# Four products at two Strassen levels in layer one's second gate/up pass, with most second-level weight sums on GpSimd

## The chip, the cores and the metric

The kernel runs on one core of a Trainium2 chip. The metric is device time of one execution in microseconds (us); lower is better.

## What is computed

Two identical layers, each an attention block without softmax (A) followed by a gated block (B), over x of 2048 rows and 1024 columns. The same weights serve both layers. Cut to what matters here:

```python
def _B_ref(x, w_gate, w_up, w_down):
    g = jnp.einsum("bsd,df->bsf", x, w_gate)   # 1024 -> 3584
    u = jnp.einsum("bsd,df->bsf", x, w_up)
    h = g * u
    return jnp.einsum("bsf,fd->bsd", h, w_down)

x = x + _A_ref(_layernorm(x), A_wqkv, A_wo)
x = x + _B_ref(_layernorm(x), B_w_gate, B_w_up, B_w_down)
x = x + _A_ref(_layernorm(x), A_wqkv, A_wo)
x = x + _B_ref(_layernorm(x), B_w_gate, B_w_up, B_w_down)
```

## The kernel before

All of it is one instruction stream per engine, written out by Python. Each operation names the bytes of SBUF and the PSUM banks that it reads and writes, and a planner turns these into semaphore waits. Every engine executes its stream in order: TensorE (PE), VectorE (DVE), ScalarE (ACT), GpSimd (POOL), and SyncE (SP), from whose queue all DMAs are issued.

In a gated block the 2048 rows are done as two halves of 1024. A half is one gate/up pass and then one down-projection. A gate/up pass runs over 14 pairs of *units*. A unit is a block of 256 columns of w_gate or of w_up, the other unit of the pair the same columns of the other matrix. The product of a unit with the half's 1024 rows is done by Strassen's scheme in Winograd's form: instead of eight block products it takes seven, called 1 to 7, each with a 512 x 128 block (or a sum of blocks) of weights and a 512 x 512 block (or a difference) of the input: four matmuls of 512 columns for each unit. The first-level weight sums (for products 5, 6, 7, 3) are made once, in layer one's first pass, stored in `w_scratch` and loaded from there afterwards.

A product of the pair can be taken at a *second level*. The blocks of both units together are then split again into seven smaller products, 14 matmuls of 256 columns instead of 8 of 512. That needs second-level sums of the weights (four 128 x 256 blocks a product, `sp`), second-level differences of the input (once a pass, `tp_ops`), and more additions while results leave PSUM. `L2SETS` says for each (layer, pass) which products are taken so: none in layer one's first pass, 1 and 5 in its second, all of 1, 5, 3, 2 in both of layer two's. Layer one's second pass makes the second-level weight sums of all four products, for itself and for layer two, and stores them in `sp_scratch`; layer two only loads them.

The order of a pass is written out by hand as a string of tokens in `ORDERS`, which is repeated for each pair. `P`, `D` and a product's number with A or B are a product's matmuls for the first or second unit; `M` are the operations that combine and multiply results into h; two digits are steps of a second-level product (`11` the first matmuls of product 1, `16`, `17` the next two; `25`, `35` an addition on DVE), `F` folds one term in. `S` makes (layer one) or loads (layer two) second-level weight sums. `Ra` and `Rb` issue the loads of one unit each, in a ring of five slots (`ring_issue`): `Ra` of a pair loads the second unit of the next pair. `T0` and `T1` are ticks, at which other work is put in; in layer one's second pass that is the layer norm of layer two for eight tiles of 128 rows (`ticks1`). A token with `'` belongs to the pair before, one with `+` to the next. The first tokens of a pass, as far as they are in `early`, are put among the last matmuls of the down-projection ahead.

Lines of the profile that matter here: matmuls of 512 columns L1037, of 256 columns L1104, of the down-projection L1312. DVE's tensor-tensor operations all have L668 (the helper `tt`), its evictions from PSUM L671 (`stt`), the joins of second-level products L1122. ACT's evictions are L1042, L1051 and, of second-level products, L1147; its copies from bank to bank L1067 and L1119. Layer norm is L432, L434 and L452 on DVE and L435, L437 on POOL. L583, L585 (DVE) and L792 (POOL) belong to the projections of block A, L800 (DVE) and L809 (POOL) to its norm. DMAs are issued at L406, transposing ones at L524.

Of the kernel before, what the change touches and what calls it, by code (L numbers as in the profile page):

```python
# [180 lines left out]
def build_kernel(nc, A_x, A_wqkv, A_wo, B_w_gate, B_w_up, B_w_down, out):  # L181
# [11 lines left out]
    NNORM = 14  # L193
    YACT = True

    L2SETS = {(False, 0): "", (False, 1): "15", (True, 0): "1532", (True, 1): "1532"}
    ORDERS = {
# [4 lines left out]
    }  # L202
# [104 lines left out]
    with ExitStack() as es:  # L307
# [97 lines left out]
        def dma(dst_ap, src_ap, wr, key, rd=()):  # L405
            P.add("sp", lambda e: e.dma_start(dst_ap, src_ap), rd=rd, wr=wr, dma_sem=key)  # L406
# [231 lines left out]
        def ring_issue():  # L638
            n = RG["n"]
            if n >= 2 * NPASS:  # L640
                return
            RG["n"] = n + 1
            o = r_slot(n)[0][0]
            ps_, u = divmod(n, NPASS)
            sl = (n + 1) % NR
            if u < NU:
                j, m = unit_jm(u)
                src = wgu_v[m][:, :, j * 256:(j + 1) * 256]
                if RG["first"] and ps_ == 0:
                    dma(vb(o, 2048).rearrange("p (k c) -> p k c", c=256), src, R(o, 4096), KRR[sl])  # L650
                else:
                    dma(vb(o + 1024, 1024).rearrange("p (k c) -> p k c", c=128), src[:, :, 0:128], R(o + 1024, 2048), KRR[sl])
                    dma(vh(o + 3072, 2048), wscr[u], R(o + 3072, 4096), KRT[sl], rd=R(V_S + u * 32, 32))
                    dma(vb(o, 512).rearrange("p (k c) -> p k c", c=128), src[:, 4:8, 128:256], R(o, 1024), KRS[sl])
                return
            q, hf = divmod(u - NU, 2)
            q = DPROD[q]
            js = slice(hf * 7, hf * 7 + 7)
            if q in "123":
                e, d = {"1": (0, 0), "2": (1, 0), "3": (1, 1)}[q]  # L660
                dma(vb(o, 7 * 512).rearrange("p (j c) -> p j c", c=512), wd_v[:, js, e, d * 512:(d + 1) * 512], r_slot(n, 0, 7168), KRR[sl])
            else:
                t = {"5": 0, "6": 1, "7": 2, "4": 3}[q]
                dma(vh(o, 7 * 512).rearrange("p (j c) -> p j c", c=512), tscr[t][:, js, :], r_slot(n, 0, 7168), KRR[sl],
                    rd=R(V_D + hf * 7 * 32, 7 * 32))

        def tt(out, a, b, op, rd, wr, prd=()):
            P.add("dve", lambda e: e.tensor_tensor(out=out, in0=a, in1=b, op=op), rd=rd, wr=wr, prd=prd)  # L668

        def stt(out, a, sc, b, rd, wr, prd=(), op1=ALU.add):  # L670
            P.add("dve", lambda e: e.scalar_tensor_tensor(out=out, in0=a, scalar=sc, in1=b, op0=ALU.mult, op1=op1), rd=rd, wr=wr, prd=prd)  # L671
# [62 lines left out]
        def wt_h(o):  # L734
            return vh(o, 512).rearrange("p (k c) -> p k c", c=128)

        def wt_n(o, h, c):
            v = vb(o + 2048 * h, 1024).rearrange("p (k c) -> p k c", c=256)[:, :, 128 * c:128 * c + 128]
            return v, _seg(o + 2048 * h, 4, 512, 256 * c, 256 * c + 256)

        def prep_s(n):
            o = r_slot(n)[0][0]
            sv = [wt_h(o + 4096 + i * 1024) for i in range(4)]
            (a11, r11), (a12, r12), (a21, r21), (a22, r22) = [wt_n(o, h, c) for c in range(2) for h in range(2)]
# [264 lines left out]
        def layer_B(lnp, nxt, first):  # L1009
            is_last = nxt is None  # L1010

            def pair(ps_, p, l2):
# [5 lines left out]
                for ab_ in range(2):  # L1018
                    n = ps_ * NPASS + 2 * p + ab_
                    o = r_slot(n)[0][0]  # L1020
                    if first and ps_ == 0:
                        w = {"1": wt_n(o, 0, 0), "2": wt_n(o, 1, 0), "4": wt_n(o, 1, 1)}
# [151 lines left out]
                    so = O_SS["3"]  # L1174
                    tt(vh(so, 1024), vh(so, 1024), vh(O_CP, 1024), ALU.add, R(so, 2048) + R(O_CP, 2048), R(so, 2048))

                def sums(g, mode):
                    if mode == "load":
                        sp_load(ps_, p, g)
                        return  # L1180
                    v, rp, rv = sp_place(ps_, p, g)
                    sp = [v[:, i].rearrange("p (b c) -> p b c", b=2) for i in range(4)]
                    ws = []
                    for u in units:
                        o_ = r_slot(u["n"])[0][0]
                        if g == "12":
                            ws.append((vb(o_ + 1024, 1024).rearrange("p (b k c) -> p b k c", b=2, k=2), R(o_ + 1024, 2048)))
                        else:
                            ws.append((vh(o_ + 3072, 2048).rearrange("p (b k c) -> p b k c", b=4, k=2)[:, 0::3], R(o_ + 3072, 1024) + R(o_ + 6144, 1024)))
                    (wA, rA), (wB, rB) = ws  # L1190
# [19 lines left out]
            def gateup(ps_, ticks, l2):  # L1210
# [7 lines left out]
                def emit(it, tk):  # L1218
# [19 lines left out]
                        c["c22"](x) if tk[1] == "5" else c["fmul"](tk[1], x)  # L1238
                    elif tk[0] == "S":
                        if not jit:  # L1240
                            c["sums"](SPG[tk[1] == "5"], "make" if first else "load")
                    elif tk[0] == "F":
                        c["fold"]()
                    elif tk[0] == "T":
# [6 lines left out]
                    else:  # L1251
# [258 lines left out]
```

## Time and profile before

| what | value |
|---|---|
| median of 3 runs | 1464.54 us (1464.37 to 1464.82) |
| the profiled execution | 1464.57 us, span 1462.8 us |
| granted TensorE clock | 1.00 |
| layer one's second gate/up pass | about 497 to 660 us of the span |
| busy in 500 to 650 us | DVE 129.58, ACT 83.85, POOL 6.97 of 150 us |
| DMA share in 500 to 650 us | 1.01 |

The views of the profile used below: the page (one line per engine, the chain that ended last), the groups of instructions by line, which give the count, the busy time and the mean of one and then the idle time before them with the instruction that ended it; the windows, with each engine's busy time in a stretch; and the timeline, one row for each instruction or run of equal ones, with its start and its length. A busy engine is not an engine at its peak: matmuls overlap, so their rate is read from the distance of their starts.

### The profile page before, as it was taken

To read this page: it belongs to the slowest core of one execution; us is meant where nothing else is said; L and a number is where in the kernel's file an instruction comes from. 1 tells how busy PE (TensorE), PEld (TensorE's weight loads), DVE (VectorE), ACT (ScalarE), POOL (GpSimd) and SP (SyncE) were. 2 spreads that over 40 slices of the span, in tenths; PEclk is the share of its full clock that TensorE was granted. 3 is DMA by queue.
4 is the path that set the end of the run, shared out by engine and by line. 5 is a ranking of instruction groups with operands and counts; after the bars stand their busy time and mean duration, and the time that the engine had idled before them with its cause. 6 is when DMAs were issued, how large, how long until landed. Compare 5 with 4: busy or idle time off the path is not lost.

```text
span 1462.8 us, 20720 instructions
## 1 busy us (share of the span) xinstructions
PE 1453.9 (99%) x7830; PEld 751.8 (51%) x7830; DVE 1090.1 (75%) x1990; ACT 572.0 (39%) x1178; POOL 225.8 (15%) x239
## 2 busy tenths in 40 slices
PE   8999999999999999999999999999999999999999
PEld 3444444444444555554444444456666446666544
DVE  7986888777757699865578769879877575777653
ACT  3332355333300255550023323567776005777400
POOL 4553632000000000000034337300000000000000
PEclk9999999999999999999999999999999999999999
DMA  6133667988875799975374337679986768888642
GB/s 230 37 94 107 138 131 188 278 259 259 279 253 190 259 274 291 281 242 187 127 231 123 106 108 152 152 211 272 284 258 199 243 221 240 263 264 241 217 167 94
DMA packets 370931, 298.11 MB, mean 204 GB/s; under 512 B 234640, under 2 KB 323472, under 8 KB 370832
## 3 DMA queue, kind: packets, MB, share of 16 engines
q1 hardware_dynamic: 370832, 296.80, 69.6%
q8 instruction: 61, 1.00, 0.3%
q14 instruction: 38, 0.31, 0.1%
HBM read 218.63 MB, written 54.53 MB: 187 GB/s over the span
## 4 chain that ended last, share of the span: by engine, by line
PE 99%; DMA 1%; DVE 0%; ACT 0%; SPq 0%; issue 0%
PE ps L1037 30%; PE ps L1312 23%; PE ps L780 15%; PE ps L1104 15%; PE ps L862 8%; PE ps L954 7%; DMA arena<-in_A_wqkv_dram 1%; PE ps L902 0%; PE ps L874 0%; SPq L406 0%; PE ps L538 0%; DVE arena L668 0%; ACT arena L540 0%; PE ps L886 0%; DVE arena L671 0%; DVE arena L960 0%
## 5 line engine op out<-in xcount | busy, mean ns | idle before, releaser
L671 DVE SCALAR_TENSOR_TENSOR arena<-ps,arena 128x512 f16<-128x512 f32 (+2 forms) x508 | 340.4, 686 | 195.1 <-PE ps L1312 140.8
L1037 PE MATMUL ps<-arena 128*128 128x512 f16 x2016 | 478.5, 379 | 0.0
L668 DVE TENSOR_TENSOR arena<-arena 128x512 f16<-128x512 f16 (+4 forms) x624 | 308.8, 520 | 54.1 <-ACT arena L1147 46.4
L1312 PE MATMUL ps<-arena 128*128 128x512 f16 (+1 forms) x1568 | 340.9, 379 | 0.0
L1037 PEld LDWEIGHTS ps<-arena 128*128 128x128 f16 (+1 forms) x2016 | 192.3, 98 | 186.7 <-ACT arena L1042 13.6
L1104 PE MATMUL ps<-arena 128*128 128x256 f16 x1960 | 259.4, 273 | 0.8 <-DVE ps L1122 0.5
L1312 PEld LDWEIGHTS ps<-arena 128*128 128x128 f16 x1568 | 153.4, 98 | 183.1
L1104 PEld LDWEIGHTS ps<-arena 128*128 128x128 f16 (+1 forms) x1960 | 190.9, 98 | 83.3 <-DVE ps L1122 3.8
L780 PE MATMUL ps<-arena 128*128 128x512 bf16 x1024 | 223.7, 379 | 3.2 <-ACT arena L540 1.1
L1042 ACT ACTIVATE arena<-ps 128x512 f16<-128x512 f32 x224 | 133.8, 597 | 110.6 <-PE ps L1037 108.6
L582 ACT ACTIVATE arena<-ps 128x512 f32<-128x512 f32 x128 | 76.4, 597 | 231.5 <-PE ps L780 220.1
L780 PEld LDWEIGHTS ps<-arena 128*128 128x128 f16 x1024 | 99.6, 98 | 122.0 <-DMA arena<-in_A_wqkv_dram 1.6
L1119 ACT COPY ps<-ps 128x256 f32<-128x256 f32 x168 | 61.8, 368 | 204.0 <-PE ps L1104 201.4
L435 POOL TENSOR_SCALAR arena<-arena 128x1 f32<-128x1 f32 x64 | 27.2, 425 | 643.0 <-DVE arena L434 643.0
L862 PE MATMUL ps<-arena 128*128 128x512 bf16 x512 | 115.4, 379 | 0.0
L954 PE MATMUL ps<-arena 128*128 128x512 bf16 x512 | 111.0, 379 | 0.0
L1067 ACT COPY ps<-ps 128x512 f32<-128x512 f32 x112 | 64.2, 573 | 90.6 <-PE ps L1037 52.4
L1122 DVE TENSOR_TENSOR ps<-ps,arena 128x256 f32<-128x256 f32 x168 | 70.7, 428 | 33.6 <-PE ps L1104 16.7
L432 DVE BATCH_NORM_STATS2 arena<-arena 128x6 f32<-128x512 bf16 x128 | 88.2, 689 | 8.2 <-DMA arena<-in_A_x_dram 6.0
L585 DVE SCALAR_TENSOR_TENSOR arena<-ps,arena 128x512 bf16<-128x512 f32 x128 | 88.5, 692 | 4.4
L809 POOL TENSOR_TENSOR arena<-arena 128x1024 f16<-128x1024 f32 x32 | 79.3, 2478 | 72.9 <-DVE arena L807 71.7
L792 POOL TENSOR_TENSOR arena<-arena 128x512 f32<-128x512 f32 x60 | 74.7, 1249 | 87.1 <-DVE arena L585 85.7
(51 smaller groups left out, 705.3 us busy)
## 6 DMA issues: line engine op xcount, KB each, us to landing
arena<-w_scratch SPq DMA_DIRECT2D x84, 512.0 KB, 5.4
arena<-t_scratch SPq DMA_DIRECT2D x32, 896.0 KB, 5.7
arena<-sp_scratch SPq DMA_DIRECT2D x56, 512.0 KB, 6.0
arena<-in_B_w_down_dram SPq DMA_DIRECT2D x24, 896.0 KB, 5.8
w_scratch<-arena SPq DMA_DIRECT2D x28, 512.0 KB, 6.6
sp_scratch<-arena SPq DMA_DIRECT2D x28, 512.0 KB, 4.1
arena<-in_A_wqkv_dram SPq DMA_DIRECT2D x12, 1024.0 KB, 8.0
arena<-in_B_w_gate_dram SPq DMA_DIRECT2D x42, 256.0 KB, 5.4
```

The source lines that it names most:

```text
L432: P.add("dve", (lambda h: lambda e: e.bn_stats(st[j][:, 6 * h:6 * h + 6], x_res[:, i, (D // 2) * h:(D // 2) * (h + 1)]))(h), rd=r_x(i, (D ...
L585: P.add("dve", lambda e: e.scalar_tensor_tensor(out=dst_ap, in0=psb(bank), scalar=0.0, in1=etmp[r], op0=ALU.max, op1=ALU.add), prd=[bank], ...
L668: P.add("dve", lambda e: e.tensor_tensor(out=out, in0=a, in1=b, op=op), rd=rd, wr=wr, prd=prd)
L671: P.add("dve", lambda e: e.scalar_tensor_tensor(out=out, in0=a, scalar=sc, in1=b, op0=ALU.mult, op1=op1), rd=rd, wr=wr, prd=prd)
L780: return [e.matmul(psb(bank), xnT[:, k, i * 128:(i + 1) * 128], w[:, k, h * 512:(h + 1) * 512], start=(k == 0), stop=(k == KT - 1)) for k ...
L809: P.add("pool", lambda e: e.tensor_tensor(out=asb[b].rearrange("p (h c) -> p h c", c=32), in0=pbuf.rearrange("p (h c) -> p h c", c=32), in ...
L862: return [e.matmul(psb(bank), xr[:, t, j * 128:(j + 1) * 128], pk[:, h, t, :], start=(t == 0), stop=(t == NST - 1)) for t in range(NST)]
L954: return [e.matmul(psb(bank), xnT[:, g, i * 128:(i + 1) * 128], wp[:, g, dh * 512:(dh + 1) * 512], start=(dh == 0 and g == 0), stop=(g == ...
L1037: P.add("pe", lambda e: [e.matmul(psb(bank), w[:, k, :], x[:, k, :], start=(start and k == 0), stop=(k == 3), skip_group_check=True) for k ...
L1042: P.add("act", lambda e: e.activation(t, psb(bank), AF.Copy, scale=SG), prd=[bank], wr=r)
L1104: P.add("pe", lambda e: [e.matmul(psb(bank)[:, 256 * half:256 * half + 256], w[:, k, :], xx[:, k, :], start=(start and k == 0), stop=(k == ...
L1312: return [e.matmul(psb(bank), hv[:, 7 * hf + k, t * 128:(t + 1) * 128], w[:, k, :], start=(start and hf == 0 and k == 0), stop=(hf == 1 an ...
```

## The change

Layer one's second pass takes products 1, 5, 3 and 2 at the second level, as layer two does, in a new order of tokens. The weight sums are no longer made for two products at once by four DVE operations of 512 columns; each product's are made on their own by four operations of 256 columns, on POOL for 1, 2 and 3 and on DVE for 5. A group of two products is stored when both are made. The tokens `S1`, `S2`, `S5`, `S3` are now one product each.

A loaded unit has another layout: block 1 lies by itself at the slot's start and is loaded first (128 KB in packets of 256 bytes, under its own semaphore), blocks 2 and 4 lie side by side (256 KB in packets of 512 bytes), and the first-level sums come third. Before, blocks 1 and 2 came first (256 KB), then the sums, then block 4 (128 KB), all blocks in packets of 256 bytes. This holds for all passes but the first.

```diff
-    L2SETS = {(False, 0): "", (False, 1): "15", (True, 0): "1532", (True, 1): "1532"}
+    L2SETS = {(False, 0): "", (False, 1): "1532", (True, 0): "1532", (True, 1): "1532"}
...
-        (False, 1): "M5A' D2B' M2B' P5B' P7B' 11 D4A' D3A' Ra M5B' 16 D3B' M3A' M4A' S5 P1A D4B' M3B' Rb 17 M4B' 51 P6A D2A M2A 56 P1B P7A T1' P5A T0 57 P6B S1+",
+        (False, 1): "17 P5A' M5A' M4A' D4B' P5B' M5B' 21 P1A D3A' M3A' D3B' Ra S3 M4B' M3B' 26 S1+ 31 P1B P6A T1 36 27 T0+ P6B 37 D2A Rb 25 P7A 35 M2A S5+ F3 51 11+ P7B D2B 56 16+ S2+ M2B D4A 57",
...
+    SUM_ENG = {"1": "pool", "2": "pool", "5": "dve", "3": "pool"}
...
-                    dma(vb(o + 1024, 1024).rearrange("p (k c) -> p k c", c=128), src[:, :, 0:128], R(o + 1024, 2048), KRR[sl])
+                    dma(vb(o, 512).rearrange("p (k c) -> p k c", c=128), src[:, 0:4, 0:128], R(o, 1024), KRS[sl])
+                    dma(vb(o + 1024, 1024).rearrange("p (k c) -> p k c", c=256), src[:, 4:8, :], R(o + 1024, 2048), KRR[sl])
                     dma(vh(o + 3072, 2048), wscr[u], R(o + 3072, 4096), KRT[sl], rd=R(V_S + u * 32, 32))
-                    dma(vb(o, 512).rearrange("p (k c) -> p k c", c=128), src[:, 4:8, 128:256], R(o, 1024), KRS[sl])
...
-        def tt(out, a, b, op, rd, wr, prd=()):
-            P.add("dve", lambda e: e.tensor_tensor(out=out, in0=a, in1=b, op=op), rd=rd, wr=wr, prd=prd)
+        def tt(out, a, b, op, rd, wr, prd=(), eng="dve"):
+            P.add(eng, lambda e: e.tensor_tensor(out=out, in0=a, in1=b, op=op), rd=rd, wr=wr, prd=prd)
...
-                        w = {q: (wt(o + 1024 * i), R(o + 1024 * i, 1024)) for i, q in enumerate("412")}
+                        w = {"1": (wt(o), R(o, 1024)), "2": wt_n(o + 1024, 0), "4": wt_n(o + 1024, 1)}
...
-                def sums(g, mode):
-                    if mode == "load":
+                made = set()
+
+                def sums(q):
+                    g = [g for g in SPG if q in g][0]
+                    if not first:
                         sp_load(ps_, p, g)
                         return
                     v, rp, rv = sp_place(ps_, p, g)
...
-                    tt(sp[0], wB[:, :, 0], wB[:, :, 1], ALU.add, rB, rp[0])
-                    tt(sp[1], sp[0], wA[:, :, 0], ALU.subtract, rp[0] + rA, rp[1])
-                    tt(sp[2], wA[:, :, 0], wB[:, :, 0], ALU.subtract, rA + rB, rp[2])
-                    tt(sp[3], wA[:, :, 1], sp[1], ALU.subtract, rp[1] + rA, rp[3])
-                    dma(spscr[2 * p + SPG.index(g)].rearrange("p (i x) -> p i x", i=4), v, rv, KSPW[g, sp_buf(ps_, p)], rd=sum(rp, []))
+                    bi = g.index(q)
+                    sp = [v[:, i, 256 * bi:256 * bi + 256].rearrange("p (k c) -> p k c", c=128) for i in range(4)]
+                    rq = [R(r[0][0] + 512 * bi, 512) for r in rp]
+                    (wA, rA), (wB, rB) = [u["w"][q] for u in units]
+                    en = SUM_ENG[q]
+                    tt(sp[0], wB[:, 0:2], wB[:, 2:4], ALU.add, rB, rq[0], eng=en)
+                    tt(sp[1], sp[0], wA[:, 0:2], ALU.subtract, rq[0] + rA, rq[1], eng=en)
+                    tt(sp[2], wA[:, 0:2], wB[:, 0:2], ALU.subtract, rA + rB, rq[2], eng=en)
+                    tt(sp[3], wA[:, 2:4], sp[1], ALU.subtract, rq[1] + rA, rq[3], eng=en)
+                    made.add(q)
+                    if all(x in made for x in g):
+                        dma(spscr[2 * p + SPG.index(g)].rearrange("p (i x) -> p i x", i=4), v, rv, KSPW[g, sp_buf(ps_, p)], rd=sum(rp, []))
...
-                early = ("11", "16", "17", "P1", "21", "26", "27", "31", "36", "37", "S1", "S5", "T0", "T1", "Ra", "Rb")
+                early = ("11", "16", "17", "P1", "21", "26", "27", "31", "36", "37", "S1", "S2", "S5", "S3", "T0", "T1", "Ra", "Rb")
```

More of the change, by code (lines that the diff above doesn't have):

```diff
@@ L735, in wt_h, with wt_n @@
             return vh(o, 512).rearrange("p (k c) -> p k c", c=128)
-        def wt_n(o, h, c):
-            v = vb(o + 2048 * h, 1024).rearrange("p (k c) -> p k c", c=256)[:, :, 128 * c:128 * c + 128]
-            return v, _seg(o + 2048 * h, 4, 512, 256 * c, 256 * c + 256)
+        def wt_n(o, c):
+            v = vb(o, 1024).rearrange("p (k c) -> p k c", c=256)[:, :, 128 * c:128 * c + 128]
+            return v, _seg(o, 4, 512, 256 * c, 256 * c + 256)
         def prep_s(n):
@@ L743, in prep_s @@
             sv = [wt_h(o + 4096 + i * 1024) for i in range(4)]
-            (a11, r11), (a12, r12), (a21, r21), (a22, r22) = [wt_n(o, h, c) for c in range(2) for h in range(2)]
+            (a11, r11), (a12, r12), (a21, r21), (a22, r22) = [wt_n(o + 2048 * h, c) for c in range(2) for h in range(2)]
             rs = [R(o + 4096 + i * 1024, 1024) for i in range(4)]
@@ L1021, in pair @@
                     if first and ps_ == 0:
-                        w = {"1": wt_n(o, 0, 0), "2": wt_n(o, 1, 0), "4": wt_n(o, 1, 1)}
+                        w = {"1": wt_n(o, 0), "2": wt_n(o + 2048, 0), "4": wt_n(o + 2048, 1)}
                         w.update({q: (wt_h(o + 4096 + 1024 * i), R(o + 4096 + 1024 * i, 1024)) for i, q in enumerate("5673")})
                     else:
-                        w = {q: (wt(o + 1024 * i), R(o + 1024 * i, 1024)) for i, q in enumerate("412")}
+                        w = {"1": (wt(o), R(o, 1024)), "2": wt_n(o + 1024, 0), "4": wt_n(o + 1024, 1)}
                         w.update({q: (wt_h(o + 3072 + 1024 * i), R(o + 3072 + 1024 * i, 1024)) for i, q in enumerate("5673")})
@@ L1181, in sums @@
                     v, rp, rv = sp_place(ps_, p, g)
[L1182 to L1190, printed above, removed]
-                    tt(sp[0], wB[:, :, 0], wB[:, :, 1], ALU.add, rB, rp[0])
-                    tt(sp[1], sp[0], wA[:, :, 0], ALU.subtract, rp[0] + rA, rp[1])
-                    tt(sp[2], wA[:, :, 0], wB[:, :, 0], ALU.subtract, rA + rB, rp[2])
-                    tt(sp[3], wA[:, :, 1], sp[1], ALU.subtract, rp[1] + rA, rp[3])
-                    dma(spscr[2 * p + SPG.index(g)].rearrange("p (i x) -> p i x", i=4), v, rv, KSPW[g, sp_buf(ps_, p)], rd=sum(rp, []))
+                    bi = g.index(q)
[10 more added lines that the diff above has]
+                        dma(spscr[2 * p + SPG.index(g)].rearrange("p (i x) -> p i x", i=4), v, rv, KSPW[g, sp_buf(ps_, p)], rd=sum(rp, []))
                 def fin(q, c):
@@ L1240, in emit @@
                         if not jit:
-                            c["sums"](SPG[tk[1] == "5"], "make" if first else "load")
+                            c["sums"](tk[1])
                     elif tk[0] == "F":
```

## The prediction

> **What bounds the kernel now.** I read the page first: how long the span is, which engine fills it, and which chain ends last.
>
> ```profile
> span 1462.8 us, 20720 instructions
> ...
> PE 1453.9 (99%) x7830; PEld 751.8 (51%) x7830; DVE 1090.1 (75%) x1990; ACT 572.0 (39%) x1178; POOL 225.8 (15%) x239
> ...
> PE 99%; DMA 1%; DVE 0%; ACT 0%; SPq 0%; issue 0%
> ```
>
> TensorE (PE) is the bound, and the chain of waits is TensorE work nearly end to end. Busy time alone doesn't say that matmuls run at their rate, so next I read the timeline of PE, where a merged row's count and the start of the row after it give the step from one matmul to the next.
>
> ```profile
> 241.43 168.51 PE L1037 MATMUL ps<-arena 128*128 128x512 f16 x780
> 409.78 1.67 PE L1312 MATMUL ps<-arena 128*128 128x512 bf16 x7
> ...
> 995.34 2.35 PE L1104 MATMUL ps<-arena 128*128 128x256 f16 x20
> 997.52 0.81 PE L1037 MATMUL ps<-arena 128*128 128x512 f16 x3
> ```
>
> 780 matmuls of 512 columns from 241.43 to 409.78 are 215.8 ns each; 20 of 256 columns from 995.34 to 997.52 are 109 ns each. So PE has no holes in these stretches, and the time falls when PE has less to do, as long as nobody makes it wait. Third, the windows: the pass that changes (500 to 650 us) and layer two's second pass, which already takes four products at two levels.
>
> ```profile
> 500.00:650.00 150.00, 150.00 (x874) 85.38 (x873) 129.58 (x290) 83.85 (x180) 6.97 (x16) 1.00 1.01 283
> 1222.00:1369.00 147.00, 147.00 (x1042) 101.85 (x1041) 112.50 (x221) 107.67 (x275) 0.00 (x0) 1.00 0.85 255
> ```
>
> The columns are the window, its length, and busy time of PE, weight loads, VectorE (DVE), ScalarE (ACT) and GpSimd (POOL), then the clock, the DMA share and GB/s. PE is full in both. In the pass that changes DVE is 86% busy, the DMA engines are full (1.01), and POOL does almost nothing.
>
> **PE's part: the gain.** Per pair of units a product at one level is 8 matmuls of 512 columns, 1.726 us; at two levels it is 14 of 256 columns, 1.526 us. Two more products in 14 pairs save 28 x 0.200 = 5.6 us. A pair's PE time goes from 40 x 0.2158 + 28 x 0.109 = 11.68 us to 24 x 0.2158 + 56 x 0.109 = 11.28 us. The profiled execution took 1464.57 us (its span plus 1.77; the median is 1464.54), so the floor is 1459.0 us, if PE never waits. The layer-two window shows that four products a pair can run without a wait; but there the second-level sums of weights come ready from memory, and here they are computed.
>
> **DVE's part.** I start from the pass that has the four products and neither sums nor layer norm.
>
> ```profile
> L671 DVE SCALAR_TENSOR_TENSOR arena<-ps,arena 128x512 f16<-128x512 f32 x91 | 60.2, 685 | 6.0 <-PE ps L1037 4.7
> L668 DVE TENSOR_TENSOR arena<-arena 128x512 f16<-128x512 f16 x65 | 27.6, 425 | 26.9 <-ACT arena L1147 25.5
> ...
> L668 DVE TENSOR_TENSOR arena<-arena 128x1024 f16<-128x1024 f16 x13 | 8.9, 681 | 0.0
> ```
>
> 147 us at 11.28 us are 13.0 pairs: seven evictions, five 512-wide tensor-tensor operations and one 1024-wide fold a pair, and 112.50/13.0 = 8.6 us of DVE. The timeline of the pass that changes gives what comes on top.
>
> ```profile
> 565.46 1.55 DVE L668 TENSOR_TENSOR arena<-arena 128x512 f16<-128x512 f16 x4
> 566.92 0.68 DVE L671 SCALAR_TENSOR_TENSOR arena<-ps,arena 128x512 f16<-128x512 f32 x1
> ...
> 569.62 0.54 DVE L452 TENSOR_SCALAR arena<-arena 128x1024 f16<-128x1024 bf16 x1
> 570.08 1.41 DVE L432 BATCH_NORM_STATS2 arena<-arena 128x6 f32<-128x512 bf16 x2
> 571.52 0.21 DVE L434 BATCH_NORM_AGGREGATE arena<-arena 128x2 f32<-128x12 f32 x1
> 571.65 0.41 DVE L1122 TENSOR_TENSOR ps<-ps,arena 128x256 f32<-128x256 f32 x1
> ```
>
> Four 512-wide sums take 1.46 us from start to start; today there are two such groups a pair (2.9 us). The change keeps four 256-wide ones (product 5): 512 columns more cost 681 - 425 = 256 ns, so 256 fewer save 0.13 us each, and the four take 0.94 us. Instructions that follow each other start before the one ahead has ended (a 0.68 us eviction ends 0.08 us into the next), so a DVE without idle does the 8.6 us in about 8.2; with the sums 9.2 us a pair. Layer norm of a tile is 571.65 - 569.62 = 2.03 us. By the tick rule and the place of T1 and T0+ in the new order, about one tile falls in each of the first seven pairs. So before any contention DVE needs 11.2 us of PE's 11.28 in these seven pairs and 9.2 in the other seven. Today the pass asks less (86%) and PE sees nothing of it.
>
> **POOL's part.** Twelve 256-wide sums a pair (products 1, 2, 3) go to an engine that was idle. Nothing shows this operation; the nearest rows are these.
>
> ```profile
> L792 POOL TENSOR_TENSOR arena<-arena 128x512 f32<-128x512 f32 x60 | 74.7, 1249 | 87.1 <-DVE arena L585 85.7
> L437 POOL TENSOR_TENSOR arena<-arena 128x1 f32<-128x1 f32 x64 | 39.9, 623 | 5.3
> L435 POOL TENSOR_SCALAR arena<-arena 128x1 f32<-128x1 f32 x64 | 27.2, 425 | 643.0 <-DVE arena L434 643.0
> ```
>
> Half of 1249 ns is 0.62 us, which I take; bounds are 0.48 (a quarter of the 1.91 us of L809 below) and 0.75. Twelve are 7.5 us a pair, 8.4 with gaps, and a layer-norm tile adds 1.05: POOL has room. What it does to DVE is the question, and the trace answers it in the attention stages.
>
> ```profile
> 60.94 0.42 DVE L583 TENSOR_SCALAR arena<-arena 128x512 f32<-128x512 f32 x1
> 61.10 1.27 POOL L792 TENSOR_TENSOR arena<-arena 128x512 f32<-128x512 f32 x1
> 61.38 0.69 DVE L585 SCALAR_TENSOR_TENSOR arena<-ps,arena 128x512 bf16<-128x512 f32 x1
> 61.99 0.66 DVE L583 TENSOR_SCALAR arena<-arena 128x512 f32<-128x512 f32 x1
> ...
> 150.50 1.91 POOL L809 TENSOR_TENSOR arena<-arena 128x1024 f16<-128x1024 f32 x1 [1.20 <-DMA arena<-arena]
> 150.53 2.96 DVE L800 TENSOR_TENSOR arena<-arena 128x1024 f32<-128x1024 bf16 x1
> 155.27 1.16 DVE L800 TENSOR_TENSOR arena<-arena 128x1024 f32<-128x1024 bf16 x1
> ...
> 193.91 1.17 DVE L800 TENSOR_TENSOR arena<-arena 128x1024 f32<-128x1024 bf16 x1
> 194.08 1.08 POOL L435 TENSOR_SCALAR arena<-arena 128x1 f32<-128x1 f32 x1 [0.81 <-DVE arena L434]
> ```
>
> At 150.53 a DVE operation with both inputs in SBUF meets a running POOL operation: it takes 2.96 us where 1.16 is its own time, so it stood still until POOL ended at 152.41. At 194.08 it is the other way round: a one-column POOL operation takes 1.08 us and ends with DVE's. The eviction at 61.38, with one input in PSUM, takes its usual 0.69 under POOL, and the single-input operation at 61.99 takes 0.66 for 0.42. So one of the two stands still for whole instructions, evictions excepted. The Trainium skill has this as a rule (SBUF — State Buffer, Who interferes with whom): a VectorE operation with two SBUF inputs and a GpSimd operation that reads SBUF exclude each other for an instruction's length. These rows agree with it.
>
> A pair has ten such DVE operations (five 512-wide ones, the fold, four sums) and the layer norm's L452 as an eleventh. POOL runs some 66 to 75% of the pair; an operation that comes at any moment waits 0.7 x 0.31 = 0.22 us on average, and one right behind another, as the four sums and the fold are, finds POOL let in between and waits longer. Bounds are 0 and 0.62 us each; I take 0.25. Then DVE needs 9.2 + 2.03 + 2.75 = 14.0 us in a layer-norm pair, 2.7 over PE's 11.28, and 9.2 + 2.5 = 11.7 in a plain one, 0.4 over: 7 x 2.7 + 7 x 0.4 = 21.7 us. Once, DVE may run late by what lies between the last join into a bank (token 17) and the bank's next use (21): 0.436 + 0.863 + 0.218 = 1.5 us. Stalls 20.2, gain 5.6: 1464.57 + 14.6 = 1479 us.
>
> How DVE reaches PE: behind a late DVE are, in its order, the two joins, M5, M3A, M4B, M3B; M3B frees the buffer that ACT fills from "31", and "36" on PE overwrites what ACT still has to read. So PE will wait at L1104 for ACT's L1147, with DVE's L671 behind it.
>
> **The rest.** ACT: the window of layer two shows it 107.67 of 147 us busy with the same products, 27% free. Loads: the bytes of a unit are the same, with half the 256-byte packets gone; where PE and DVE are slower than DMA this is worth nothing, and in layer two's window PE is already full. The second-level input differences of products 2 and 3 (eight 512-wide operations, once) fall in the down-projection ahead; at 0.34 us each they are 2.7 us of a DVE that runs ahead of need there: zero, or 2.7 us at worst.
>
> **The rivals.** *POOL falls where DVE evicts* (faster): the order puts S3 and S1 beside the evictions of M3 to M5. If waits stay under 0.06 us an operation, stalls are below 7 x 0.6 - 1.5 = 2.7 us and the time is 1459 to 1461.6 us. For it: seven of DVE's operations a pair are evictions, which don't wait. Against: POOL needs 8.4 of 11.3 us, so it can't avoid the other half.
>
> *Waits about 0.1 us each*: layer-norm pairs take 12.3 us, 7.3 over in all, less 1.5: stalls eat the gain, 1464 to 1466 us.
>
> *The load loop binds*: the next pair's first block is loaded behind the store of the sums.
>
> ```profile
> 561.98 0.33 SPq L406 DMA_DIRECT2D sp_scratch<-arena  x1
> 562.35 0.45 SPq L406 DMA_DIRECT2D arena<-in_B_w_up_dram  x1
> ```
>
> ```profile
> arena<-in_B_w_gate_dram SPq DMA_DIRECT2D x11, 128.0 KB, 5.3
> ```
>
> S2 ends on POOL, SP issues the store and then the load (0.4 us apart), whose 128 KB block of today takes 5.3 us to land; S1 (four sums with gaps, 2.8), layer norm (1.05 at most), S2 (2.8) follow: 12.3 us, against 11.28. With 12.3 in seven pairs and 11.3 in the seven without layer norm the pass is 165.2 us, 1.6 more than the 163.6 of today's 14 x 11.68; as POOL stands behind DVE too, 1465 to 1470 us.
>
> *The change doesn't do what it says* has no room: 392 matmuls more at L1104 follow from the set of products alone.
>
> **How the numbers follow.** A measurement can tell 0.2% (2.9 us). Forecast, stalls from the lock, 1468 to 1500 us: 0.65. Load loop as the leading cause: 0.12, of which 0.04 within 0.2%. Waits of 0.1: 0.08, half within and half above. Faster: 0.15. So faster 0.15, within 0.08, slower 0.77. The range runs from 1460 (the faster rival) to 1496, which is a wait of 0.37 us an operation; waits above 0.4 are left out, since a slowed pair thins POOL out.
>
> **What would show it.** Right: L1104 x2352, L1037 x1792; PE idle before L1104 in the pass, 1.5 to 3 us in its first seven pairs and under 1 us later; L668 512-wide means up from 425 ns; DVE above 95% of the pass; POOL's 256-wide operations at 0.5 to 0.75 us. Wrong: L668 at its old times beside POOL; POOL idle before S1 with a DMA as releaser and DVE idle too (the loop); holes in PE only at the pass's start; or no holes at all.

## The result and the profile after

The changed kernel takes 1485.48 us (median of 4 runs, 1484.87 to 1486.09) where the kernel before took 1464.68 in the same comparison: a ratio of 1.0142, 95% interval 1.0124 to 1.0159. It is 20.8 us slower. Forecast were 14.6 us slower, 1479, with a range of 1460 to 1496. The profiled execution took 1485.86 us.

In the changed kernel nearly every line stands one lower than before: L668 is now L669 (VectorE's tensor-tensor operations, and now GpSimd's too), L671 is L672, L1037 is L1038, L1104 is L1105, L1122 is L1123, L1147 is L1148. The page of the changed kernel:

```profile
span 1484.1 us, 21488 instructions
...
PE 1453.9 (98%) x7933; PEld 763.9 (51%) x7998; DVE 1130.8 (76%) x2012; ACT 594.7 (40%) x1276; POOL 343.6 (23%) x407
...
PE 90%; DVE 8%; issue 1%; DMA 1%; ACT 0%; SPq 0%; DVEq 0%
```

The chain that ended last was TensorE to 99%; now 8% of it is VectorE. Over the whole span VectorE is only 76% busy, which says nothing here: the 8% lie in one pass, between 495 and 680 us, where VectorE is 58% of the chain. The groups show the move of work from 512 to 256 columns as forecast (1792 and 2352 matmuls) and a new idle time, 19.1 us before the second-level matmuls, ended by the joins on VectorE:

```profile
L1038 PE MATMUL ps<-arena 128*128 128x512 f16 x1792 | 428.7, 379 | 0.0
L1105 PE MATMUL ps<-arena 128*128 128x256 f16 x2352 | 304.9, 274 | 19.1 <-DVE ps L1123 18.2 <-DVE arena L672 0.3
```

The windows of the changed kernel: the pass from 500 to 660 us, then six pairs with layer norm, then three without it.

```profile
500.00:660.00 160.00, 143.00 (x958) 89.49 (x957) 154.16 (x278) 97.64 (x250) 108.62 (x160) 0.99 0.86 249
...
505.88:591.18 85.30, 73.37 (x480) 45.08 (x481) 83.05 (x151) 49.26 (x126) 55.47 (x85) 0.98 0.86 245
604.00:641.92 37.92, 34.81 (x240) 22.61 (x241) 35.99 (x65) 24.59 (x63) 26.21 (x36) 1.00 0.92 275
```

VectorE is 154.16 of 160 us busy (96%), TensorE 143.00. The groups of VectorE by shape in 500 to 660 us say with what:

```profile
L672 DVE SCALAR_TENSOR_TENSOR arena<-ps,arena 128x512 f16<-128x512 f32 x84 | 54.2, 678 | 1.0 <-PE ps L1105 1.0
L669 DVE TENSOR_TENSOR arena<-arena 128x512 f16<-128x512 f16 x60 | 34.6, 585 | 4.6 <-ACT arena L1148 3.2
L669 DVE TENSOR_TENSOR arena<-arena 128x256 f16<-128x256 f16 x48 | 29.9, 661 | 0.4
...
L669 DVE TENSOR_TENSOR arena<-arena 128x1024 f16<-128x1024 f16 x12 | 12.4, 1033 | 0.0
...
L453 DVE TENSOR_SCALAR arena<-arena 128x1024 f16<-128x1024 bf16 x8 | 5.4, 670 | 0.0
```

An eviction, with one input in PSUM, takes its old 0.68 us. Whatever reads two inputs from SBUF has grown: 585 ns for 425, 1033 for 681. One operation with a single input, layer norm's L453, has grown too, 0.67 us for 0.54; the forecast counted it in. The timeline of one pair with layer norm shows where that reaches TensorE:

```profile
585.58 0.21 DVE L435 BATCH_NORM_AGGREGATE arena<-arena 128x2 f32<-128x12 f32 x1
...
585.88 0.28 POOL L436 TENSOR_SCALAR arena<-arena 128x1 f32<-128x1 f32 x1 [3.22 <-DVE arena L435]
...
586.81 5.75 POOL L669 TENSOR_TENSOR arena<-arena 128x256 f16<-128x256 bf16 x8
586.93 3.85 DVE L669 TENSOR_TENSOR arena<-arena 128x256 f16<-128x256 f16 x5
...
588.20 1.03 PE L1038 MATMUL ps<-arena 128*128 128x512 f16 x4
...
590.71 0.75 DVE L1123 TENSOR_TENSOR ps<-ps,arena 128x256 f32<-128x256 f32 x2
591.18 1.16 PE L1105 MATMUL ps<-arena 128*128 128x256 f16 x8 [1.95 <-DVE ps L1123]
```

GpSimd stood 3.22 us at its first layer-norm operation (L436), which waits for VectorE's aggregate; behind it lay S2 and S3, and all eight sums then ran in one burst. At the same moment VectorE came to S5's four sums and the fold F3 (the row x5), which alternate with the burst and take 3.85 us. The two joins of step `56` are queued behind them, and TensorE stands at `57` until they are done.

### The profile page after: what moved, and what is told of

It is laid out like the page before. It is cut to its first block, busy times and chain, and to the rows that moved or that the text cites. A ratio compares the mean times of both kernels' runs of the same rounds, so it can differ in the third digit from the quotient of the medians.

```text
span 1484.1 us, 21488 instructions
## 1 busy us (share of the span) xinstructions
PE 1453.9 (98%) x7933; PEld 763.9 (51%) x7998; DVE 1130.8 (76%) x2012; ACT 594.7 (40%) x1276; POOL 343.6 (23%) x407
## 2 busy tenths in 40 slices
DMA packets 327929, 298.18 MB, mean 201 GB/s; under 512 B 148624, under 2 KB 280464, under 8 KB 327824
## 4 chain that ended last, share of the span: by engine, by line
PE 90%; DVE 8%; issue 1%; DMA 1%; ACT 0%; SPq 0%; DVEq 0%
PE ps L1038 23%; PE ps L1314 23%; PE ps L781 15%; PE ps L1105 14%; PE ps L863 7%; PE ps L955 7%; DVE arena L669 4%; DVE arena L672 2%; DVE ps L1123 1%; DVE arena L433 1%; DMA arena<-in_A_wqkv_dram 1%; PE ps L875 0%; PE ps L903 0%; DVE arena L453 0%; ACT arena L1148 0%
## 5 line engine op out<-in xcount | busy, mean ns | idle before, releaser
L672 DVE SCALAR_TENSOR_TENSOR arena<-ps,arena 128x512 f16<-128x512 f32 (+2 forms) x522 | 348.2, 685 | 192.0 <-PE ps L1314 138.2
L1038 PE MATMUL ps<-arena 128*128 128x512 f16 x1792 | 428.7, 379 | 0.0
L669 DVE TENSOR_TENSOR arena<-arena 128x512 f16<-128x512 f16 (+4 forms) x632 | 343.8, 568 | 59.6 <-ACT arena L1148 51.7
L1105 PE MATMUL ps<-arena 128*128 128x256 f16 x2352 | 304.9, 274 | 19.1 <-DVE ps L1123 18.2
L1105 PEld LDWEIGHTS ps<-arena 128*128 128x128 f16 (+1 forms) x2352 | 225.5, 98 | 116.3 <-DVE ps L1123 35.5
L1038 PEld LDWEIGHTS ps<-arena 128*128 128x128 f16 (+1 forms) x1792 | 169.7, 98 | 163.8 <-ACT arena L1043 13.6
L669 POOL TENSOR_TENSOR arena<-arena 128x256 f16<-128x256 bf16 (+1 forms) x168 | 118.2, 727 | 267.5 <-DMA arena<-in_B_w_up_dram 263.2
L1148 ACT ACTIVATE arena<-ps 128x256 f16<-128x256 f32 x336 | 112.4, 390 | 32.0 <-PE ps L1105 30.3
L436 POOL TENSOR_SCALAR arena<-arena 128x1 f32<-128x1 f32 x64 | 27.7, 432 | 278.9 <-DVE arena L435 278.9
```

The lines of the kernel that those rows point to most:

```text
L669: P.add(eng, lambda e: e.tensor_tensor(out=out, in0=a, in1=b, op=op), rd=rd, wr=wr, prd=prd)
L1038: P.add("pe", lambda e: [e.matmul(psb(bank), w[:, k, :], x[:, k, :], start=(start and k == 0), stop=(k == 3), skip_group_check=True) for k ...
L1105: P.add("pe", lambda e: [e.matmul(psb(bank)[:, 256 * half:256 * half + 256], w[:, k, :], xx[:, k, :], start=(start and k == 0), stop=(k == ...
L1148: P.add("act", lambda e: e.activation(dst, src, AF.Copy, scale=SG), prd=[bk], wr=rd_)
```

## The experiments

Three theories were put against each other. *The lock*: the sums on GpSimd make VectorE's two-SBUF-input operations stand still, VectorE falls behind, and its joins hold TensorE. *The load only*: the pass simply holds more work than VectorE can do, so the fewer sums VectorE has, the better. *The loads*: the loop of loads, sums and store is too long, whoever makes the sums.

**The sums left out.** GpSimd writes zeros (a memset of 256 columns) where it made the sums, behind the same waits; the sums of products 1, 2 and 3 are missing from the result.

```diff
-                    tt(sp[0], wB[:, 0:2], wB[:, 2:4], ALU.add, rB, rq[0], eng=en)
...
+                    for i in range(4):
+                        if en == "pool":
+                            P.add("pool", (lambda i: lambda e: e.memset(sp[i], 0.0))(i), rd=ins[i], wr=rq[i])
```

> POOL's twelve sums a pair are left out: POOL writes zeros of the same size to the same places instead, with the same waits, and reads nothing. DVE's work is that of the changed kernel. Theory 1: L669 at 425 ns, DVE needs 9.2 us in a plain pair and 11.2 in one with layer norm, PE's holes nearly go: 1459 to 1463 us. Theory 2: 1483 to 1487 us, as DVE's instructions are the same. Theory 3: POOL's operations are shorter, so the loop is too: 1459 to 1463 us as well.

1460.30 us (ratio 0.9969, 0.9953 to 0.9985). The window of this kernel, and its groups by shape in it:

```profile
500.00:660.00 160.00, 159.65 (x1114) 108.66 (x1113) 141.94 (x316) 109.50 (x283) 48.46 (x166) 1.00 0.99 287
```

```profile
L669 DVE TENSOR_TENSOR arena<-arena 128x512 f16<-128x512 f16 x70 | 28.9, 420 | 11.5 <-ACT arena L1148 10.1
...
L669 DVE TENSOR_TENSOR arena<-arena 128x256 f16<-128x256 f16 x52 | 12.7, 286 | 1.3 <-DMA arena<-w_scratch 0.7
L669 DVE TENSOR_TENSOR arena<-arena 128x1024 f16<-128x1024 f16 x14 | 9.6, 683 | 0.0
```

TensorE is full again, and the time is the forecast's floor (1459.0) within 1.3 us: the four products do save what was forecast if nothing waits. GpSimd is still 48.46 us busy, but with operations that only write, and VectorE has its own times: 420, 286, 683 ns. The same five operations of VectorE that took 3.85 us above take 1.61 here; the join then even waits for TensorE:

```profile
581.46 1.61 DVE L669 TENSOR_TENSOR arena<-arena 128x256 f16<-128x256 f16 x5
583.30 0.76 DVE L1123 TENSOR_TENSOR ps<-ps,arena 128x256 f32<-128x256 f32 x2 [0.23 <-PE ps L1105]
...
584.18 1.04 PE L1105 MATMUL ps<-arena 128*128 128x256 f16 x8
```

These rows are from its timeline. The sums cost 1485.5 - 1460.3 = 25.2 us by their reading and their length alone. This kernel doesn't tell these two apart, since a memset is also shorter than a sum: 316 ns in the mean for 727.

**The sums all on VectorE.**

```diff
-    SUM_ENG = {"1": "pool", "2": "pool", "5": "dve", "3": "pool"}
+    SUM_ENG = {"1": "dve", "2": "dve", "5": "dve", "3": "dve"}
```

> All sixteen second-level weight sums on DVE, POOL makes none. Theory 1 (exclusion: DVE's operations with two SBUF inputs stand still under POOL's): L669's 512-wide operations go back from 568 to about 425 ns, DVE gets 12 x 0.235 = 2.8 us of sums a pair and loses about 2.5 us of standing still, so the time stays near the changed kernel's, 1480 to 1488 us. Theory 2 (plain load: DVE just has too much to do, POOL does it no harm): 14 pairs x 2.8 us on top, about 1520 us. Theory 3 (the load loop through S1 and S2 on POOL binds): POOL's part of the loop gets shorter, below 1475 us.

1485.42 us (1.0139, 1.0110 to 1.0169), as long as the changed kernel. In 500 to 660 us:

```profile
L669 DVE TENSOR_TENSOR arena<-arena 128x256 f16<-128x256 f16 x120 | 30.4, 286 | 2.2 <-DMA arena<-w_scratch 0.5
L669 DVE TENSOR_TENSOR arena<-arena 128x512 f16<-128x512 f16 x60 | 24.4, 417 | 2.8 <-ACT arena L1148 1.6
```

Now no operation is stretched, and VectorE is busy all the same (153.40 of 160 us) since it does the sums. Moving twelve sums a pair to GpSimd costs VectorE as much in standing still as doing them costs. That refutes the load alone, by which VectorE's own sums had to be much the dearer. It says little of the loads: with VectorE this full, a loop of loads that had become shorter would not show in the time. The Trainium skill (Perfetto Trace Analysis, Optimizing Scalar/DVE Operations) warns that offloading between these two engines might not help, since they share a read port; the pair 1485.5 and 1485.4 us agrees.

**The lock by itself.** In the kernel before, layer two's second pass has the same four products and room on VectorE. Twelve additions a pair that nobody needs are put on GpSimd there, and in a second kernel twelve memsets of the same width instead.

```diff
+                        for i in range(6 if ps_ == 1 else 0):
+                            P.add("pool", lambda e: e.tensor_tensor(out=vh(O_XN[1], 256), in0=v[:, 0, 0:256], in1=v[:, 1, 0:256], op=ALU.add), rd=sum(rp, []), wr=R(O_XN[1], 512))
```

> The kernel before, with POOL operations added that nobody needs, in layer two's second pass: twelve 256-wide additions a pair, which read the second-level sums as they are loaded and write to an unused buffer. DVE is 76% busy there and has six operations with two SBUF inputs a pair. Theory 1: L668's means in that pass rise from 425 (512 wide) and 681 ns (1024 wide) by 0.1 to 0.3 us, evictions (L671) stay at 685; DVE has room for 6 x 0.25 = 1.5 us a pair, so the time stays within 2 us of 1464.7. Theory 2: no duration of DVE changes.

> As the probe before, with twelve 256-wide writes of zeros a pair on POOL that read nothing. Theory 1, in the form that only operations that read SBUF exclude DVE's second input: L668 stays at 425 and 681 ns. If any POOL operation does: as with the additions, though less, since they are shorter.

With additions 1466.90 us (1.0014, 1.0003 to 1.0024); with memsets 1465.09 in one run, beside 1465.00 for the kernel before. The groups of the first in 1222 to 1369 us, then those of the second:

```profile
L671 DVE SCALAR_TENSOR_TENSOR arena<-ps,arena 128x512 f16<-128x512 f32 x91 | 60.0, 682 | 1.2
L668 DVE TENSOR_TENSOR arena<-arena 128x512 f16<-128x512 f16 x64 | 36.9, 577 | 25.0 <-ACT arena L1147 23.6
L668 DVE TENSOR_TENSOR arena<-arena 128x1024 f16<-128x1024 f16 x13 | 9.5, 733 | 0.0
...
L1182 POOL TENSOR_TENSOR arena<-arena 128x256 f16<-128x256 f16 x150 | 105.1, 701 | 47.2 <-DMA arena<-sp_scratch 35.7
```

```profile
L668 DVE TENSOR_TENSOR arena<-arena 128x512 f16<-128x512 f16 x66 | 28.1, 425 | 28.7 <-ACT arena L1147 27.3
L668 DVE TENSOR_TENSOR arena<-arena 128x1024 f16<-128x1024 f16 x13 | 8.9, 681 | 0.0
L1182 POOL MEMSET arena<- 128x256 f16 x150 | 46.7, 311 | 108.9 <-DMA arena<-sp_scratch 100.3
```

Additions stretch VectorE's sums from 425 to 577 ns and leave evictions as they were; memsets do nothing. The rule of the Trainium skill (SBUF — State Buffer, Who interferes with whom) that a GpSimd operation which only writes doesn't contend with a VectorE operation of two SBUF inputs is borne out. The memsets are shorter than the additions (311 ns for 701), but length alone doesn't explain it: they fill 32% of the time and leave the mean where it was. Where VectorE has room, 12 additions a pair cost 1.9 us in all, not 25.

**S5 ahead of the burst.** If the wait is S5 standing between the burst and the join, moving S5 to an earlier place should free the join.

```diff
-  ... 31 P1B P6A T1 36 ... M2A S5+ F3 51 ...
+  ... 31 P1B S5 P6A T1 36 ... M2A F3 51 ...
```

> Only the token S5+ moves: it becomes S5 of the pair itself and stands ahead of P6A and T1, where POOL in the changed kernel's trace has ended S1 and waits for layer norm. Theory 1: the four sums take about 1 us instead of 3.1, so DVE wins 2 us a pair: 1460 to 1472 us. Theory 2: same operations, 1483 to 1487 us. Theory 3: unchanged, 1483 to 1487 us.

1481.55 us (1.0113, 1.0083 to 1.0142): far above what was expected. The waits of this kernel in 490 to 690 us, and its groups in 500 to 660:

```profile
PE ps L1105 <- ACT arena L1130: 14.4, 10, 2.3
```

```profile
L669 DVE TENSOR_TENSOR arena<-arena 128x512 f16<-128x512 f16 x62 | 38.0, 627 | 1.3
L669 DVE TENSOR_TENSOR arena<-arena 128x256 f16<-128x256 f16 x50 | 23.2, 503 | 0.4
L669 DVE TENSOR_TENSOR arena<-arena 128x1024 f16<-128x1024 f16 x13 | 13.7, 1054 | 0.0
```

The 256-wide sums wait less (503 for 661 ns), the 512-wide ones more (627 for 585), and TensorE now waits for an eviction on ScalarE at another step. The waits add up to (627 - 420) x 62 + (503 - 286) x 50 + (1054 - 683) x 13 = 28.5 us in 12.5 pairs, 2.3 us a pair, against 2.7 in the changed kernel by the same sum. The copy on ScalarE for which TensorE waits (L1130) is itself late behind VectorE: at 573.06 the copy ahead of it waited 2.52 us for an eviction on L672. So S5 is where the loss shows, not what makes it.

**Layer norm spread.** A tick at every third unit instead of two in four, so that the tiles reach into the later pairs.

```diff
-                if u % 4 < 2 and not is_last and nxt.t_next < 8:
+                if u % 3 == 0 and not is_last and nxt.t_next < 8:
```

> The eight layer-norm tiles of the pass come at every third tick, so that they spread over all 14 pairs instead of the first seven to nine. Theories 1 and 2 (DVE's sum over the pass counts, and every pair is over PE's time): the holes even out at about 1.9 us a pair and the time stays within 3 us of 1485. If only the crowded pairs hurt (a rival for theory 1's plain pairs): below 1475 us.

1487.05 us (1.0150, 1.0121 to 1.0180). It wins nothing: there is no room in the plain pairs into which layer norm could go. That it is 1.6 us slower than the changed kernel says nothing, since its granted clock fell in three stretches of about 8 us, the changed kernel's in one (last section).

**The layout without the products.** The new layout of a unit and the sums product by product, but products 1 and 5 and the order of the kernel before; first with all sums on VectorE, then with those of 1, 2 and 3 on GpSimd.

```diff
-    L2SETS = {(False, 0): "", (False, 1): "1532", (True, 0): "1532", (True, 1): "1532"}
+    L2SETS = {(False, 0): "", (False, 1): "15", (True, 0): "1532", (True, 1): "1532"}
...
-        (False, 1): "17 P5A' M5A' M4A' ...",
+        (False, 1): "M5A' D2B' M2B' P5B' P7B' 11 D4A' D3A' Ra M5B' 16 D3B' M3A' M4A' S5 S3 P1A D4B' M3B' Rb 17 M4B' 51 P6A D2A M2A 56 P1B P7A T1' P5A T0 57 P6B S1+ S2+",
...
-    SUM_ENG = {"1": "pool", "2": "pool", "5": "dve", "3": "pool"}
+    SUM_ENG = {"1": "dve", "2": "dve", "5": "dve", "3": "dve"}     # the first of the two only
```

> Of the change only the units' layout and the sums made for each product by itself, all on DVE; products (1 and 5) and order as before. DVE has sixteen 256-wide sums instead of eight 512-wide ones a pair, some 0.8 us more: 9.6 us plain, 11.6 with layer norm, PE's 11.68. All theories: within 3 us of 1464.7; if the new packets of the loads are worth anything in any pass, below 1464.

> As the one before, with the sums of 1, 2 and 3 on POOL as in the change; still two products, old order. Theory 1: DVE's operations with two SBUF inputs get longer (512 wide above 500 ns, 256 wide above 450), but DVE has only six of them a pair and 6.8 us of work of its own, so with standing still some 9 us plain and 11 with layer norm: no holes, 1464 to 1466 us. It is the exclusion together with a full DVE that costs, not the exclusion alone. If POOL's sums come late by themselves (theory 3): 1470 us or more.

On VectorE 1464.66 us (0.9999, 0.9990 to 1.0008): the layout, with its fewer and longer packets, is worth nothing, as forecast. On GpSimd 1468.94 (1.0029, 1.0018 to 1.0039), 3 us more than expected, although VectorE is less busy. The window of the second, its group of second-level matmuls, and its timeline in one pair:

```profile
500.00:650.00 150.00, 147.36 (x850) 82.27 (x849) 119.93 (x230) 83.04 (x176) 111.51 (x172) 1.00 0.97 277
```

```profile
L1105 PE MATMUL ps<-arena 128*128 128x256 f16 x348 | 53.6, 273 | 2.6 <-DVE ps L1123 2.6
```

```profile
592.80 2.29 DVE L669 TENSOR_TENSOR arena<-arena 128x256 f16<-128x256 f16 x4
595.02 0.68 DVE L672 SCALAR_TENSOR_TENSOR arena<-ps,arena 128x512 f16<-128x512 f32 x1
595.73 0.80 DVE L669 TENSOR_TENSOR arena<-arena 128x512 f16<-128x512 f16 x1
596.46 0.42 DVE L1123 TENSOR_TENSOR ps<-ps,arena 128x256 f32<-128x256 f32 x1
```

VectorE is 80% busy and TensorE waits all the same: S5's four sums take 2.29 us instead of about 1.02 (beside memsets, in the kernel without sums), one more sum 0.80 instead of 0.43, and the join behind them is late. The lock costs latency, not only VectorE's time.

**Three products.** From the kernel before, only product 3 is added at the second level; sums stay on VectorE, two products at once. VectorE then has room, TensorE's floor is 1461.8 us (14 x 0.200 less). The second kernel adds the spread ticks of above.

```diff
-    L2SETS = {(False, 0): "", (False, 1): "15", ...
+    L2SETS = {(False, 0): "", (False, 1): "153", ...
-        (False, 1): "M5A' D2B' M2B' P5B' P7B' 11 D4A' ...",
+        (False, 1): "M5A' 31' D2B' M2B' 36' P5B' 37' P7B' 35' F3' 11 D4A' ...",
```

> The kernel before, with one product more at two levels (1, 5 and 3) in layer one's second pass, its steps put among the tokens of the order before; the weight sums stay two groups of 512-wide operations on DVE, POOL makes none. PE: 14 x 0.2 = 2.8 us less. DVE: one 512-wide addition and the fold more, 0.9 us a pair: 9.7 us plain and 11.7 with layer norm, against PE's 11.48. Theory 1: no exclusion, and at most 7 x 0.26 us over: 1461.5 to 1464 us.

> As the one before, with the layer norm's tiles at every third tick over the whole pass: 9.7 + 1.2 = 10.9 us of DVE a pair on average, below PE's 11.48. Theory 1: 1461.5 to 1463 us, no holes in PE.

1480.36 us (1.0105, 1.0088 to 1.0122) and 1480.00 (1.0101, 1.0086 to 1.0116): both missed. The waits of the first in 490 to 690 us:

```profile
PE ps L1104 <- DVE ps L1122: 5.6, 19, 0.3
PE ps L1104 <- ACT arena L1147: 3.6, 14, 0.3
```

No engine is full here (VectorE 139.62 of 160 us); TensorE waits three times a pair, about 0.3 us each by this view and 0.42 to 0.47 by the distance of the matmuls' starts, for VectorE's join (19 waits) or ScalarE's eviction (14) of a step that was placed too close ahead. 14 pairs of 1.3 us on the floor of 1461.8 make 1480. So the order itself has a price. Two more orders were tried, the second with the ticks spread:

```diff
# the first
+        (False, 1): "M5A' 31' D2B' M2B' P5B' 36' P7B' 37' 11 D4A' M4A' 35' F3' M5B' D3A' Ra 16 D4B' M3A' D3B' M4B' S5 P1A M3B' Rb 17 51 P6A D2A M2A 56 P1B P7A T1' P5A T0 57 P6B S1+",
# the second
+        (False, 1): "M5A' D2B' S5 M2B' P5B' 31' D4A' M4A' 11 36' P7B' 16 37' M5B' 35' F3' D3A' M3A' Ra P1A D4B' D3B' Rb 17 M4B' M3B' 51 P6A D2A M2A 56 P1B P7A T1' P5A T0 57 P6B S1+",
```

> Products 1, 5 and 3 at two levels as in the first try, sums as before on DVE, with the steps 31, 36 and 37 further apart (0.86 us or more of other matmuls between them and between 16, P1A and 17), since the first try's holes are PE waiting for ACT's evictions of these steps, not for a full DVE. Theory 1 with that reading: holes below 0.3 us a pair, 1462 to 1467 us. If the three products don't fit beside the rest whatever the order: 1475 us or more.

> Products 1, 5 and 3 at two levels, sums on DVE in two groups, layer norm at every third tick, and an order in which each step of a second-level product is followed by at least 0.65 us of other matmuls before the step that needs its eviction: D4A' and 11 between 31' and 36', P7B' and 16 between 36' and 37', 37' and D3A' between 16 and P1A; S5 stands early. Theory 1 (DVE has 10.9 us a pair for PE's 11.48 and no exclusion; the first tries' holes were order): 1462 to 1466 us. If a DVE this full delays some join in any order: 1470 us or more.

1485.23 us (1.0139, 1.0124 to 1.0154) and 1466.74 (1.0013, 1.0004 to 1.0022). The first is worse than what it should mend: there TensorE also waits 13 times for VectorE's sums (L668), 6.1 us in all. The second comes within 5 us of its floor and still isn't faster than the kernel before. Its window:

```profile
500.00:650.00 150.00, 148.00 (x942) 88.72 (x940) 139.50 (x311) 97.19 (x229) 7.08 (x16) 1.00 0.94 274
```

VectorE is at 93% and six joins come 0.3 us late. No kernel that makes all the sums came out measurably below the kernel before; whether another order of three products would is open.

## Why the prediction was right in sign and short in size

**PE's gain** held. With the sums left out the kernel takes 1460.3 us, where the floor was put at 1459.0.

**The lock** held, in kind and in price. From the rows of the changed kernel and those with memsets, VectorE's waits in 160 us are (585 - 420) x 60 + (661 - 286) x 48 + (1033 - 683) x 12 = 32 us. 48 sums of product 5 are 12 pairs, so 2.7 us a pair, or 0.27 for each of the ten operations; 0.25 was taken. It is unevenly spread, 0.17 for one that comes alone and 0.38 for those that follow each other, as the forecast said of the four sums. GpSimd's sums take 727 ns in the mean, their own waits for VectorE included; 0.62 was taken for one alone. Beside evictions, with no wait to be seen, single ones take 0.66 to 0.67 (at 577.94 and 593.79).

**Layer-norm pairs** held. From the matmul row at 505.88 to that at 591.18 are six pairs: 14.2 us each where 14.0 was forecast. Of the 0.2, most is one pair in which the granted clock fell (below).

**Plain pairs failed.** The window 604.00 to 641.92 is three pairs, 12.6 us each where 11.7 was forecast. The sum of VectorE's work took VectorE to be without idle. The timeline of the changed kernel shows one plain pair:

```profile
616.78 1.16 PE L1105 MATMUL ps<-arena 128*128 128x256 f16 x8 [1.21 <-DVE ps L1123]
...
620.21 9.20 POOL L669 TENSOR_TENSOR arena<-arena 128x256 f16<-128x256 bf16 x12 [3.30 <-DMA arena<-in_B_w_up_dram]
...
622.29 0.94 DVE L669 TENSOR_TENSOR arena<-arena 128x512 f16<-128x512 f16 x1
...
623.51 0.54 DVE L669 TENSOR_TENSOR arena<-arena 128x512 f16<-128x512 f16 x1 [0.27 <-ACT arena L1148]
...
624.53 0.43 DVE L669 TENSOR_TENSOR arena<-arena 128x512 f16<-128x512 f16 x1 [0.49 <-ACT arena L1148]
...
625.57 3.31 DVE L669 TENSOR_TENSOR arena<-arena 128x256 f16<-128x256 f16 x5
...
629.28 0.39 PE L1105 MATMUL ps<-arena 128*128 128x256 f16 x2 [0.92 <-DVE ps L1123]
```

VectorE waits 0.52 + 0.12 + 1.70 = 2.3 us longer than with memsets, near the forecast's 2.5. But it also stands idle 0.27 + 0.49 us until ScalarE has evicted what the next sum reads. With memsets it is idle at the same two sums, 0.33 + 0.60 us, at no cost, since TensorE is full there. 9.2 + 2.3 + 0.8 is 12.3 of the 12.5 us of this pair.

So the period of a plain pair is set by a loop over three engines, not by VectorE's work: a late join delays TensorE, TensorE delays the evictions, and these delay VectorE's next sums. From the start of `57` (616.78) to S5 (625.57) are 8.79 us, against 8.57 with memsets (572.89 to 581.46). S5 and F3 hold the joins up for 3.24 us, until 628.81, against 1.61. The next `57` starts 0.47 us after the joins do. These are the 12.50 us. The chain that ended last agrees: from 604 to 630 us it is TensorE's matmuls to 61% and VectorE's sums to 25%, while in the layer-norm pair above, from 583 to 592 us, no engine but VectorE stands in it. That a lock can hold TensorE while VectorE has a fifth of its time free was seen by itself in the layout experiment. From 591.18 on, six pairs lose (12.57 - 11.28) x 6 = 7.7 us (the row of the sixth, at 666.59, is not shown), where 7 x 0.4 = 2.8 was forecast.

**The slack** was placed wrongly. 1.5 us, worked out from a join of `17` and the use of its bank at `21`, was taken off. The place that waits is `57`, right behind the joins of `56`; it starts 0.47 us after they do (590.71 and 591.18), before the second has ended. With memsets the joins start at 583.30 and `57` at 584.18, 0.41 us later than it could; before that VectorE waited 0.23 us. So there are 0.64 us, and a plain pair has them each time: it loses (8.79 - 8.57) + (3.24 - 1.61) - 0.64 = 1.2 us, which is what the pair shown lost (12.50 - 11.28). The pass's first pair lost only 1.0 us and its last one nothing that the waits show, where the forecast had 2.7 + 0.4 - 1.5 = 1.6 for these two; whether that is a slack or the other work at the pass's ends can't be told from these rows.

**Where TensorE waits** was wrong. Forecast was `36`, waiting for ScalarE's L1147 with the M operations late behind VectorE. By the order, only `16` and D4A's four matmuls of 512 columns stand between `56` and `57`, and S5 and F3 stand ahead of the joins of `56` on VectorE's queue: the operations that suffer most from the lock lie directly before the join that is needed soonest. In the layer-norm pairs the price didn't depend on it, since VectorE's work set it there; in the plain pairs it did, by the loop above.

Together: six layer-norm pairs lose 17.6 us, six plain ones 7.7, the first and the last 1.0: 26.3, and the profiled execution is 26.9 above the floor of 1459.0. Forecast were 16.2, 2.4 and 1.6: 20.2. Of the 6.1 us between, 5.3 are the plain pairs, the term that was mis-sized; 1.4 are in the layer-norm pairs, -0.6 at the ends.

**The rivals.** The faster one (GpSimd falls beside the evictions) is refuted by the means of 585 to 1033 ns. Waits of 0.1 us are refuted by 0.27. The loop of loads doesn't lead: VectorE is busy 83.05 of 85.30 us in the layer-norm pairs, and in the plain pair it is VectorE's joins that TensorE waits for. But the loads have a part that wasn't seen: a load holds GpSimd (3.30 us above), and the twelve sums behind it then come in one burst of 9.20 us, over S5. How much a more even GpSimd would win was not tried. Two readings of the forecast were off without effect. Not half but two thirds of a unit's 256-byte packets are gone: the pages count 234640 packets under 512 bytes before and 148624 after, 1024 fewer of 1536 for each of 84 loads of a unit. And 14 x 11.68 is 163.5, not 163.6.

## What to carry to other kernels

Before moving elementwise work from VectorE to GpSimd, count the VectorE operations that read two inputs from SBUF and will run beside it: here twelve 0.7 us sums a pair cost ten such operations 2.7 us, as much as VectorE would have spent on the sums. Then look for the dependency that follows such a group most closely, since the wait is paid as latency there even when VectorE has time left. And put an order that has been tuned to the next step's eviction through the same reading when a product is added: four kernels with one product more ran 2 to 20 us slower although VectorE had room.

## What the runs showed of the hardware

The lock is selective to a degree that the rows of the kernel before couldn't show: GpSimd memsets 32% of the time cost VectorE nothing (425 ns), additions of the same width, 71% of the time, 152 ns an operation. Between back-to-back short operations the two engines alternate, one operation each (VectorE starts at 586.93, 587.66, 588.29, 588.96 and 589.63, GpSimd in between at 587.55, 588.17, 588.85 and 589.52): five of VectorE, 1.61 us alone, took 3.85 us beside eight of GpSimd. GpSimd lost little by it: its eight took 5.75 us, 0.72 each for 0.66 to 0.67 alone. And the granted clock, 1.00 in all the windows read before, fell in one pair of the changed kernel:

```profile
534.00:540.00 6.00, 5.93 (x34) 3.97 (x35) 4.92 (x11) 2.69 (x7) 4.22 (x7) 0.72 0.50 138
```

The window is that pair's first 6 us; the pair took 15.0 us where its neighbours took 14.1. In this pass the clock fell in two more runs, twice with S5 ahead of the burst (532 to 540 and 572 to 580 us) and three times with layer norm spread. These are the three kernels in which TensorE stands still for some 2 us at a time (2.0 to 2.3 us the longest wait, 0.6 or less in the others). Whether that is the cause, no run here shows.
